# Four common steps of 208 columns in place of three of 256 between the forms of an attention and mixture-of-experts kernel

## The chip, the cores and the metric

The kernel runs on one core of a Trainium2 chip. The metric is device time in microseconds (us) of one execution, as the median of several runs. Engines are named as in the profile: PE is TensorE (PEld its weight loads), DVE is VectorE, ACT is ScalarE, POOL is GpSimd, SP is SyncE.

## What is computed

Attention of 4 x 8 heads over 768 positions with 64 numbers a head, with a window of 96 positions and 8 global ones, is followed by a top-1 routed mixture of 8 experts. All is float32. The second part matters here:

```
logits = x @ w_gate                      # x: 3072 tokens x 512
expert_idx = argmax(logits, axis=1)
for e in range(8):
    xe = x[expert_idx == e]
    h = maximum(xe @ w1[e], 0)           # w1[e]: 512 x 1024
    ye = h @ w2[e]                       # w2[e]: 1024 x 512
    out[expert_idx == e] = gate_w * ye
```

How many tokens an expert gets is known only when the kernel runs. With 3072 tokens it is 384 in the mean.

## The kernel before, in words

Every operation is first recorded in a list (`Flow.record`, L47), with what it reads and writes. `Flow.derive` finds from these which earlier operations each one must wait for, and `Flow.play` emits all of them in order, each on its engine's queue with its semaphore waits (`emit`, L239). The order within a queue is thus the order in which the Python code calls.

Attention runs over 24 blocks of 128 tokens and ends at about 205 us of the profile. Then come the experts, in the order 0, E, 1, 2, ..., 7. E is a late group of up to 128 tokens of expert 0, computed plainly (`plain`, L920).

**The two halves of an expert.** Up to 512 tokens of an expert are held as two halves of 256 columns each. Both matrix products are made as a 2 x 2 block product with seven block products in place of eight (`seven`, L836): `one`, `two`, `three`, `four`, `five`, `six`, `last`. Sums of weight blocks (`w_sums`, t1 to t4) and of token blocks (`x_sums`, `h_sums`) are made on DVE beforehand. `up` (L899) calls `seven` twice (j = 0 and 1, steps 0 to 6 and 7 to 13), `down` (L911) once (from step 14). A step writes one bank of PSUM: two column halves t times 2 (up) or 4 (down) blocks k, so 4 or 8 products, each 128 x 128 weights by up to 256 columns (`product`, L826).

After a step an engine takes the result out of PSUM: ACT copies `one` to p1 (L855); DVE adds p1 and `two` to u2 (L859); ACT activates `three` to block c11 (L864); DVE adds u2 and `four` to u3 (L870); DVE adds u3 and `five` to c22 (L874), u3 and `six` to c21 (L879), u2 and `last` to c12 (L884), and ACT activates these in place (L851). Banks come in two sets of three, X, Y and W, and consecutive calls of `seven` take turns: `one` and `three` write X, `two`, `four` and `six` write Y, `five` and `last` write W. So `four` waits until u2 has read Y, `six` until u3 has, and `last` until c22 has read W. Two more banks (`tbanks`) serve the transposes of `y_out`.

**Forms.** Columns past an expert's token count are wasted. So TensorE's instructions from a certain step on exist in 17 forms, for 128, 136, ..., 256 columns (`SIZES`, L636): `forms` opens such a section, and `emit_forms` (L269) writes it 17 times within a `Switch`, in which TensorE jumps to the form that fits. Only TensorE's instructions have forms; those of other engines are emitted once, for all 256 columns of each half. A form's products differ only in how many columns they take (`_dyn`, L257). A hint (`f.hint`) ahead of the section names the form that will be taken, and the branch itself is recorded at L275.

Between the end of one expert's form and the beginning of the next there is a **common part**, without forms and so with all 256 columns. In `group` (L1207), for each of the experts 1 to 7, it holds in this order: the hint; the loads of the next expert's rows (SP); `one`; two `y_out` of the expert before (4 transposes on TensorE each, then a scaling on ACT, then a send by POOL); `two`; two more `y_out`; `three`. Expert 1 has only one `y_out` there, since the late group precedes it. Then the form begins with `four`.

Other work is attached to steps with `at_(i, ...)` and is recorded after step i: weight sums on DVE after steps 0 and 1 (`own[3]`, `own[4]`, `own[5]`; L702, L699, L700), `pads` of the expert after the next after step 3 (four indirect DMAs on POOL, L744), the next weights' DMAs (SP) from step 14 on. Token sums of the next expert and its `marks` are recorded at the very end of an expert, so that on DVE they, and the two sums of step 0, stand ahead of u2.

Of the kernel before, what the change touches and what calls it, by code (L numbers as in the profile page):

```python
# [24 lines left out]
class Flow:  # L25
# [5 lines left out]

    RINGS = {"SP": 24, "POOL": 20, "ACT": 8}

    def __init__(self, tc):
# [9 lines left out]

    def record(self, engine, name, args, kw):  # L47
        reads, writes = list(kw.pop("_r", ())), list(kw.pop("_w", ()))
        dyn = kw.pop("_dyn", False)
        first = True  # L50
        for key, a in [(None, a) for a in args] + list(kw.items()):
            if not isinstance(a, bass.AP):
                first = first and key is not None
                continue
            if a.space == bass.MemoryType.DRAM:
                first = False
                continue
            (writes if key in ("out", "accum_out") or (key is None and first) else reads).append(a)
            first = False
        here = sys._getframe(2)  # L60
        self.ops.append(dict(e=engine, name=name, args=args, kw=kw, r=reads, w=writes, dyn=dyn,
                             form=self.form, dma="dma" in name,
                             at=(here.f_code.co_filename, here.f_lineno)))

# [171 lines left out]
        for j in op["need"]:  # L236
            self.engines[op["e"]].wait_ge(sems[self.ops[j]["proc"]], self.ops[j]["level"])

    def emit(self, op, sems, n):  # L239
        self.wait(op, sems)  # L240
        args, kw = op["args"], op["kw"]
        if op["name"] == "await":
            return
        if op["name"] == "number":
            ap, label = args
            self.loads[label] = self.nc.values_load(
                ap, min_val=0, max_val=1, skip_runtime_bounds_check_because="a comparison's result")
            return
        if op["name"] == "load":
            index, n, label = args  # L250
            self.loads[label] = self.nc.tensor.value_load(index, min_val=0, max_val=n - 1)
            return
        if op["name"] == "hint":
            index, n, label = args
            self.hints[label] = self.loads[label], self.nc.tensor.switch_hint(self.loads[label], n, label)
            return
        if n is not None and op["dyn"]:  # L257
            args = tuple(a[:, 0:n] for a in args[:1]) + tuple(args[1:])
            kw = dict(kw, rhs=kw["rhs"][:, 0:n])
        call = getattr(self.engines[op["e"]], op["name"])  # L260
        where = dict(call=call, args=args, kw=kw)

        exec(_code(*op["at"]), where)
        if op["dma"]:
            where["inst"].then_inc(sems[op["proc"]], 16)
        elif op.get("told"):
            where["inst"].then_inc(sems[op["proc"]], 1)

    def emit_forms(self, form, body, sems):  # L269
        index, sizes, label = form  # L270
        pe = self.nc.tensor
        choose, rest = body[0], body[1:]
        self.wait(choose, sems)
        r, label = self.hints[label]
        for f in pe.Switch(r, len(sizes), hint=label):  # L275
            for op in rest:
                self.emit(op, sems, sizes[f])


class _Recorder:  # L280
# [344 lines left out]
class Experts:  # L625
# [6 lines left out]

    P, E, CAP, LATE = 128, 8, 512, 128
    SIZES = list(range(128, 257, 8))  # L636

    def __init__(self, f, dims, psum, keep, wsets, work, zeros, ylast):
# [149 lines left out]
    def bank(self):  # L788
        self.tp ^= 1
        return self.psum[:, self.tbanks[self.tp], :].rearrange("p (c t) -> p c t", c=4)  # L790
# [32 lines left out]
            in_=self.y[j], in_offset=None, bounds_check=self.out.shape[0] - 1, oob_is_err=False, **kw)  # L823


    def product(self, bank, w, x, fresh, half=None):  # L826

        f, n = self.f, len(w)
        for t in range(2):
            for k in range(n):  # L830
                f.pe.matmul(self.psum[:, bank, 256 * t:256 * t + 256], lhsT=w[k][:, ts(t, 128)], rhs=x[k],  # L831
                            start=(fresh and t == 0 and k == 0), stop=True, skip_group_check=True, _dyn=True)
            if half and t == 0:
                half()

    def seven(self, c, a, s, cols, order, dst, act, half=None):  # L836

        f, V = self.f, self.f.dve
        X, Y, W = self.sets[self.turn]
        p1, u2, u3 = self.p1[self.turn], self.u2[self.turn], self.u3[self.turn]  # L840
        self.turn ^= 1

        def bank(b):
            return self.psum[:, b, :].rearrange("p (t c) -> p t c", t=2)

        def mm(b, wq, xq, fresh, half=None):
            self.product(b, [c[wq][:, k, cols] for k in order], [xq[:, k, :] for k in order], fresh, half)

        def relu(d):
            if act:  # L850
                f.act.activation(d, d, act)  # L851

        def one():
            mm(X, "b11", a["a11"], True)
            f.act.copy(p1, bank(X))  # L855

        def two():
            mm(Y, "t2", s[1], True)
            V.tensor_tensor(u2, p1, bank(Y), ALU.add)  # L859

        def three():
            mm(X, "b21", a["a12"], False, half)
            if act:
                f.act.activation(dst["c11"], bank(X), act)  # L864
            else:
                f.act.copy(dst["c11"], bank(X))

        def four():
            mm(Y, "t3", s[2], True)
            V.tensor_tensor(u3, u2, bank(Y), ALU.add)  # L870

        def five():
            mm(W, "t1", s[0], True)
            V.tensor_tensor(dst["c22"], u3, bank(W), ALU.add)  # L874
            relu(dst["c22"])

        def six():
            mm(Y, "t4", a["a22"], True)
            V.tensor_tensor(dst["c21"], u3, bank(Y), ALU.add)  # L879
            relu(dst["c21"])  # L880

        def last():
            mm(W, "b22", s[3], False)
            V.tensor_tensor(dst["c12"], u2, bank(W), ALU.add)  # L884
            relu(dst["c12"])

        return [one, two, four, five, six, three, last] if half else [one, two, three, four, five, six, last]

    def h_sums(self, j):
        V, sh = self.f.dve, self.sh  # L890
# [8 lines left out]
    def up(self, e):  # L899

        c, xt, h = self.quarters(e, True), self.xt, self.h
        a = dict(a11=xt[:, 0:2, 0], a12=xt[:, 2:4, 0], a21=xt[:, 0:2, 1], a22=xt[:, 2:4, 1])
        s = [self.sx[:, j] for j in range(4)]
        steps = []
        for j in range(2):
            k, k2 = slice(2 * j, 2 * j + 2), slice(4 + 2 * j, 6 + 2 * j)
            dst = dict(c11=h[:, k, 0], c12=h[:, k2, 0], c21=h[:, k, 1], c22=h[:, k2, 1])
            steps += self.seven(c, a, s, slice(256 * j, 256 * j + 256), (0, 1), dst, AF.Relu)
        return steps

    def down(self, e, half=None):  # L911
# [32 lines left out]
def kernel(  # L944
# [60 lines left out]
    with ExitStack() as stack:  # L1005
# [201 lines left out]
        def group(p):  # L1207
# [6 lines left out]
            def at_(i, *fns):  # L1214
                todo.setdefault(i, []).extend(fns)

            def run(steps, first):
                for i, fn in enumerate(steps, first):
                    fn()
                    for fn in todo.pop(i, ()):  # L1220
                        fn()

            ups = ex.up(g) if g != E else None
            if p:

                prev = order[p - 1]
                if E not in (g, prev):
                    f.hint(*forms[g])
                if nxt is not None and g != E:
                    ex.load_x(nxt, [f"pad{nxt}.{j}" for j in range(4)])  # L1230
                if nxt is None:
                    f.number(keep["flag"][0:1, 0:1], "redo")
                outs = [0] if prev == E else [1, 3, 0, 2]
                own = ex.w_sums(g, True) + ex.w_sums(g, False) if ups else None
                if ups:
                    at_(0, own[3], own[4])
                    at_(1, own[5])
                    run(ups[:1], 0)
                for j in outs[:2]:
                    ex.y_out(prev, j)  # L1240
                if ups:
                    run(ups[1:2], 1)
                for j in outs[2:]:
                    ex.y_out(prev, j)
                if ups:
                    run(ups[2:3], 2)
            D = 14
            if g != E:

# [39 lines left out]
            else:  # L1289
# [7 lines left out]
                    at_(D + 6, xs[2], xs[3], lambda: ex.marks(nxt))  # L1297
                if after is not None:
                    pieces = ex.w_pieces(after)
                    at_(3, lambda: ex.pads(after))  # L1300
                    at_(D, *pieces[:4])
                    at_(D + 6, *pieces[4:])

# [1 line left out]
                ex.plain(0, lambda i: [fn() for fn in todo.pop(i, ())])  # L1305
                return
            with f.forms(*forms[g]):
                run(ups[3:] if p else ups[2:], 3 if p else 2)
                early = ((1, "act"), (3, "dve")) if nxt is None else ()
                run(ex.down(g, (lambda: [ex.y_out(g, j, on) for j, on in early]) if early else None), D)  # L1310
            assert not todo, todo
# [432 lines left out]
```

## Time and profile before

| | |
|---|---|
| median of 14 runs | 513.77 us (512.78 to 514.45) |
| the profiled execution | 514.43 us, its span 512.6 us |
| TensorE's mean granted clock | 0.985 |
| busy: POOL | 164.8 us (32%) |

By stages, from the view of busy times in windows, in us:

| stage (us) | length | PE | DVE | ACT | POOL | DMA share |
|---|---|---|---|---|---|---|
| 223.5 to 264.4, expert 1 | 40.90 | 40.90 | 25.75 | 8.29 | 5.54 | 0.75 |
| 264.4 to 302.5, expert 2 | 38.10 | 38.10 | 29.32 | 9.65 | 8.77 | 0.67 |
| 302.5 to 343.3, expert 3 | 40.80 | 40.80 | 29.33 | 9.76 | 9.17 | 0.61 |
| 343.3 to 381.4, expert 4 | 38.10 | 38.10 | 29.39 | 9.65 | 9.41 | 0.66 |
| 381.4 to 423.5, expert 5 | 42.10 | 42.10 | 29.32 | 9.76 | 9.38 | 0.60 |
| 423.5 to 464.25, expert 6 | 40.75 | 40.75 | 29.33 | 9.76 | 5.07 | 0.29 |
| 464.25 to 499.4, expert 7 | 35.15 | 33.55 | 23.71 | 10.80 | 6.32 | 0.09 |
| 499.4 to 512.6, the end | 13.20 | 0.00 | 0.74 | 0.22 | 1.94 | 0.08 |

How to read the lines that follow: a group names the line, the engine, the operation, what it writes and reads, the shape and the count; then busy time and the mean of one in ns; then the idle time ahead of it and what ended most of that. One product in float32 leaves two matmul records. A matmul's length is modelled and overlaps the next, so the pace is read from starts.

### The profile page before, as it was taken

Reading aid. Unit: us, or ns where it says so; the run is one execution under the profiler, and the core shown is the slowest. Engines: PE = TensorE matmul, PEld = TensorE weight load, DVE = VectorE, ACT = ScalarE, POOL = GpSimd, SP = SyncE. Lnnn points to the kernel's source line nnn. Section 1 sums busy time; section 2 is a strip of 40 time slices with the busy share of each in tenths; the row PEclk is TensorE's granted clock in tenths of the full one; section 3 lists DMA queues with packets and bytes.
Section 4 is the critical chain, followed back from the end, with each engine's and each line's share of the span. In section 5 each row is a group of like instructions: output and inputs, shape, how many; then the busy total and the mean of one; then the engine's idle time right before and its main releaser. Section 6 shows DMA issues by size and latency. Waiting matters only on the chain. (4 is left out here: it accounts for less than half of the span.)

```text
span 512.6 us, 10727 instructions
## 1 busy us (share of the span) xinstructions
PE 481.2 (94%) x4397; PEld 452.6 (88%) x4397; DVE 350.7 (68%) x612; ACT 171.8 (34%) x292; POOL 164.8 (32%) x192
## 2 busy tenths in 40 slices
PE   3999999999986999999999999999999999999990
PEld 3888888888875899899999999999999999999880
DVE  4655675897885785566777886777876776777840
ACT  3766655555552130312113213204213203302410
POOL 1544456667765053322006006007007003003011
PEclk9999999999999799999999999999999999999996
DMA  9999999998425347998756665657567469001000
GB/s 151 206 241 253 195 201 239 262 223 185 104 103 126 131 158 149 203 241 206 164 187 155 142 211 137 130 170 178 134 195 183 108 161 231 2 2 59 9 24 29
DMA packets 120344, 79.24 MB, mean 155 GB/s; under 512 B 86422, under 2 KB 103318, under 8 KB 120272
## 3 DMA queue, kind: packets, MB, share of 16 engines
q1 hardware_dynamic: 112960, 63.77, 56.6%
q0 software_dynamic: 6480, 14.45, 7.9%
q8 instruction: 51, 0.84, 0.7%
q14 instruction: 21, 0.17, 0.1%
q10 hardware_dynamic: 832, 0.02, 0.1%
HBM read 61.39 MB, written 23.71 MB: 166 GB/s over the span
## 5 line engine op out<-in xcount | busy, mean ns | idle before, releaser
L831 PE MATMUL psum<-arena 128*128 128x208 f32 (+5 forms) x1776 | 298.3, 329 | 5.0 <-DVE arena L795 4.1
L831 PEld LDWEIGHTS psum<-arena 128*128 128x128 f32 x1776 | 287.6, 191 | 10.5 <-DVE arena L795 4.2
L821 POOL DMA_INDIRECT out_dram<-arena,to x16 | 20.8, 1297 | 214.9 <-ACT arena L813 189.9
L491 DVE TENSOR_TENSOR arena<-psum,arena 128x1024 f32<-128x1024 f32 x40 | 48.8, 1219 | 30.9 <-PE psum L481 30.9
L499 ACT ACTIVATE arena<-arena 128x1024 f32<-128x1024 f32 (+1 forms) x48 | 47.4, 987 | 46.6 <-DVE arena L491 42.0
L505 POOL TENSOR_TENSOR arena<-arena 128x512 f32<-128x512 f32 x40 | 53.2, 1332 | 29.7 <-ACT arena L499 29.7
L851 ACT ACTIVATE arena<-arena 128x512 f32<-128x512 f32 x48 | 30.2, 630 | 63.5 <-DVE arena L874 43.2
L481 PE MATMUL psum<-arena 64*128 64x128 f32 x704 | 48.5, 284 | 1.2 <-ACT arena L467 0.7
L481 PEld LDWEIGHTS psum<-arena 64*128 64x128 f32 x704 | 43.4, 191 | 5.8 <-issue 3.2
L855 ACT COPY arena<-psum 128x512 f32<-128x512 f32 x24 | 14.0, 584 | 90.1 <-PE psum L831 90.0
L518 PE MATMUL psum<-arena 128*64 128x128 f32 x704 | 43.7, 276 | 0.3 <-issue 0.3
L518 PEld LDWEIGHTS psum<-arena 128*64 128x64 f32 x704 | 37.9, 137 | 3.2 <-issue 0.4
L870 DVE TENSOR_TENSOR arena<-arena,psum 128x512 f32<-128x512 f32 x24 | 16.5, 688 | 27.0 <-PE psum L831 26.9
L617 POOL DMA_INDIRECT xg_dram<-arena,slot_i x24 | 24.6, 1027 | 29.4 <-DVE arena L884 21.8
L744 POOL DMA_INDIRECT xg_dram<-small,pad x24 | 25.5, 1061 | 12.5 <-issue 7.0
L884 DVE TENSOR_TENSOR arena<-arena,psum 128x512 f32<-128x512 f32 x24 | 16.5, 688 | 17.6 <-PE psum L831 17.6
L874 DVE TENSOR_TENSOR arena<-arena,psum 128x512 f32<-128x512 f32 x24 | 16.5, 688 | 16.7 <-PE psum L831 16.7
L879 DVE TENSOR_TENSOR arena<-arena,psum 128x512 f32<-128x512 f32 x24 | 16.5, 688 | 15.2 <-PE psum L831 15.2
L821 POOL DMA_INDIRECT out_dram<-ylast,to x17 | 17.3, 1015 | 22.7 <-ACT ylast L813 14.6
L457 PE MATMUL psum<-ident,arena 128*128 128x128 f32 x96 | 16.1, 294 | 8.7 <-DMA arena<-in_k_dram 7.2
L859 DVE TENSOR_TENSOR arena<-arena,psum 128x512 f32<-128x512 f32 x24 | 16.4, 685 | 11.1 <-PE psum L831 10.7
L699 DVE TENSOR_TENSOR arena<-arena 128x1024 f32<-128x1024 f32 x16 | 19.6, 1227 | 2.8 <-DMA arena<-in_moe_w_dram 2.8
(148 smaller groups left out, 529.1 us busy)
## 6 DMA issues: line engine op xcount, KB each, us to landing
arena<-in_moe_w_dram SPq DMA_DIRECT2D x64, 512.0 KB, 5.6
arena<-xg_dram SPq DMA_DIRECT2D x64, 128.0 KB, 6.1
arena<-in_q_dram SPq DMA_DIRECT2D x24, 256.0 KB, 5.7
arena<-in_k_dram SPq DMA_DIRECT2D x24, 256.0 KB, 5.7
arena<-in_v_dram SPq DMA_DIRECT2D x24, 256.0 KB, 5.8
xg_dram<-arena SPq DMA_DIRECT2D x2, 1032.0 KB, 5.7
xg_dram<-arena,slot_i POOLq DMA_INDIRECT x24, 4.2
xg_dram<-small,pad POOLq DMA_INDIRECT x24, 3.2
```

Of the source, the lines that this page charges most:

```text
L481: f.pe.matmul(self.psum[:, 2 * g + a, c:c + P], lhsT=kt[r, m, :], rhs=qt[r, m, :], start=True, stop=True, skip_group_check=True)
L491: f.dve.tensor_tensor(e, s, self.bias[:, g, :, 1:3, :].rearrange("p h k c -> p h (k c)"), ALU.add)
L499: f.act.activation(e, e, AF.Exp)
L505: f.pool.tensor_tensor(self.es[n % 3][:, g], e[:, :, 0:P], e[:, :, P:2 * P], ALU.add)
L518: f.pe.matmul(po[r, m, :], lhsT=self.v[(n - ab) % 6][:, 2 * m + a, :], rhs=self.e[n % 2][:, m // 2, 2 * a + m % 2, P * ab:P * ab + P], sta ...
L617: self.f.pool.indirect_dma_start(out=self.xs[:], out_offset=bass.IndirectOffsetOnAxis(ap=k["slot_i"][:, b % 2, u:u + 1], axis=0), in_=self ...
L699: return [lambda: V.tensor_tensor(c["t3"], c["b22"], c["b12"], ALU.subtract), lambda: V.tensor_tensor(c["t1"], c["b12"], c["b11"], ALU.sub ...
L744: self.f.pool.indirect_dma_start(out=self.xs[:], out_offset=bass.IndirectOffsetOnAxis(ap=self.keep["pad"][:, g, j:j + 1], axis=0), in_=sel ...
L821: return pool.indirect_dma_start(out=self.out[:], out_offset=bass.IndirectOffsetOnAxis(ap=self.keep["to"][:, g, j:j + 1], axis=0), in_=sel ...
L831: f.pe.matmul(self.psum[:, bank, 256 * t:256 * t + 256], lhsT=w[k][:, ts(t, 128)], rhs=x[k], start=(fresh and t == 0 and k == 0), stop=Tru ...
L851: f.act.activation(d, d, act)
L870: V.tensor_tensor(u3, u2, bank(Y), ALU.add)
```

## The change

The common part gets `four` as its fourth step, and its four steps take the first 208 columns (`COMMON`) of each half. A form with more columns than 208 begins with `rest`: the products of `one`, `two`, `three` and `four` for the columns past 208, into banks of the other set and one of the transposes' banks. In a form of up to 208 these products are left out (`_past`); what they would have told other engines is told by the next product that is emitted (`more`). The other engines have no forms: for the columns 208 to 255 ACT makes one more copy and one more activation, and DVE two more additions, in every expert from 1 on, and they are recorded ahead of `five`. Expert 0, the second call of `seven` in `up` and the call in `down` stay as they were. `pads` are attached to step 4 in place of step 3.

```diff
@@ record
-        dyn = kw.pop("_dyn", False)
+        dyn, past = kw.pop("_dyn", False), kw.pop("_past", 0)
@@ emit(self, op, sems, n, more=0)
         if n is not None and op["dyn"]:
+            n -= op["past"]
             args = tuple(a[:, 0:n] for a in args[:1]) + tuple(args[1:])
             kw = dict(kw, rhs=kw["rhs"][:, 0:n])
...
-        elif op.get("told"):
-            where["inst"].then_inc(sems[op["proc"]], 1)
+        elif op.get("told") or more:
+            where["inst"].then_inc(sems[op["proc"]], int(bool(op.get("told"))) + more)
@@ emit_forms
         for f in pe.Switch(r, len(sizes), hint=label):
+            more = 0
             for op in rest:
-                self.emit(op, sems, sizes[f])
+                if op["past"] and sizes[f] <= op["past"]:
+                    self.wait(op, sems)
+                    more += bool(op.get("told"))
+                    continue
+                self.emit(op, sems, sizes[f], more)
+                more = 0
@@ Experts
-    P, E, CAP, LATE = 128, 8, 512, 128
+    P, E, CAP, LATE, COMMON = 128, 8, 512, 128, 208
@@ product(self, bank, w, x, fresh, half=None, cut=slice(0, 256))
-                f.pe.matmul(self.psum[:, bank, 256 * t:256 * t + 256], lhsT=w[k][:, ts(t, 128)], rhs=x[k],
-                            start=(fresh and t == 0 and k == 0), stop=True, skip_group_check=True, _dyn=True)
+                f.pe.matmul(self.psum[:, bank, 256 * t + cut.start:256 * t + cut.stop], lhsT=w[k][:, ts(t, 128)],
+                            rhs=x[k][:, cut], start=(fresh and t == 0 and k == 0), stop=True,
+                            skip_group_check=True, _dyn=True, _past=cut.start)
@@ seven(..., half=None, common=False)
+        X2, Y2, W2 = self.sets[self.turn ^ 1]
+        some, past = slice(0, self.COMMON if common else 256), slice(self.COMMON, 256)
...
         def one():
-            mm(X, "b11", a["a11"], True)
-            f.act.copy(p1, bank(X))
+            mm(X, "b11", a["a11"], True, cut=some)
+            f.act.copy(p1[:, :, some], bank(X)[:, :, some])
...
         def four():
-            mm(Y, "t3", s[2], True)
-            V.tensor_tensor(u3, u2, bank(Y), ALU.add)
+            mm(Y, "t3", s[2], True, cut=some)
+            V.tensor_tensor(u3[:, :, some], u2[:, :, some], bank(Y)[:, :, some], ALU.add)
+
+        def rest():
+            T = self.tbanks[self.tp ^ 1]
+            mm(X2, "b11", a["a11"], True, cut=past)
+            f.act.copy(p1[:, :, past], bank(X2)[:, :, past])
+            mm(Y2, "t2", s[1], True, cut=past)
+            V.tensor_tensor(u2[:, :, past], p1[:, :, past], bank(Y2)[:, :, past], ALU.add)
+            mm(W2, "b11", a["a11"], True, cut=past)
+            mm(W2, "b21", a["a12"], False, cut=past)
+            f.act.activation(dst["c11"][:, :, past], bank(W2)[:, :, past], act)
+            mm(T, "t3", s[2], True, cut=past)
+            V.tensor_tensor(u3[:, :, past], u2[:, :, past], bank(T)[:, :, past], ALU.add)
...
-        return [one, two, four, five, six, three, last] if half else [one, two, three, four, five, six, last]
+        if half:
+            return [one, two, four, five, six, three, last]
+        if common:
+            return [one, two, three, four, lambda: [rest(), five()], six, last]
+        return [one, two, three, four, five, six, last]
@@ up
-            steps += self.seven(c, a, s, slice(256 * j, 256 * j + 256), (0, 1), dst, AF.Relu)
+            steps += self.seven(c, a, s, slice(256 * j, 256 * j + 256), (0, 1), dst, AF.Relu,
+                                common=(e > 0 and j == 0))
@@ group
                 if ups:
-                    run(ups[2:3], 2)
+                    run(ups[2:4], 2)
...
-                    at_(3, lambda: ex.pads(after))
+                    at_(4, lambda: ex.pads(after))
...
-                run(ups[3:] if p else ups[2:], 3 if p else 2)
+                run(ups[4:] if p else ups[2:], 4 if p else 2)
```

`two` and `three` change as `one` does.

## The prediction

> **What bounds the kernel now.** I read the page's part 1 and part 2 first, then the matmul group of its part 5, to see which engine the time belongs to.
>
> ```profile
> PE 481.2 (94%) x4397; PEld 452.6 (88%) x4397; DVE 350.7 (68%) x612; ACT 171.8 (34%) x292; POOL 164.8 (32%) x192
> ...
> PE   3999999999986999999999999999999999999990
> ...
> L831 PE MATMUL psum<-arena 128*128 128x208 f32 (+5 forms) x1776 | 298.3, 329 | 5.0 <-DVE arena L795 4.1
> ```
>
> TensorE is busy in every slice, and the expert products of L831 are most of it. They waited 5.0 us in all, 4.1 of it in the first expert, which the change doesn't touch. So time here is TensorE's pace times its columns. TensorE's granted clock is 1.00 in each of these stretches. The pace comes from starts in the timeline of TensorE from 225 us on (start, length, what, records; a merged line bears the shape of its first record). One product is two records, so a step of 4 products in the up half is 8 records.
>
> ```profile
> 267.00 1.89 PE L831 MATMUL psum<-arena 128*128 128x256 f32 x8
> 268.73 1.04 PE L810 MATMUL psum<-ident,arena 128*128 128x128 f32 x8
> 269.60 34.82 PE L831 MATMUL psum<-arena 128*128 128x256 f32 x216
> 304.25 1.04 PE L810 MATMUL psum<-ident,arena 128*128 128x128 f32 x8
> ...
> 386.59 38.78 PE L831 MATMUL psum<-arena 128*128 128x256 f32 x216
> 425.21 1.04 PE L810 MATMUL psum<-ident,arena 128*128 128x128 f32 x8
> ```
>
> A step of 256 columns takes 268.73 - 267.00 = **1.73 us** (216 ns a record). The stretch 269.60 to 304.25 is `three`, 200 records in the form and the next expert's `one`: (34.65 - 2 x 1.73) / 200 = 156 ns. In the same way 386.59 to 425.21 gives 176 ns, and the stretch between these, 307.73 to 345.02, 169 ns. Which width each form has is in the groups with shapes kept apart; over experts 1 to 7 these are
>
> ```profile
> L831 PE MATMUL psum<-arena 128*128 128x208 f32 x400 | 70.7, 339 | 0.0
> L831 PE MATMUL psum<-arena 128*128 128x200 f32 x400 | 68.0, 332 | 0.0
> L831 PE MATMUL psum<-arena 128*128 128x184 f32 x400 | 62.7, 319 | 0.0
> L831 PE MATMUL psum<-arena 128*128 128x136 f32 x200 | 24.7, 283 | 0.9 <-DVE arena L859 0.8
> ```
>
> Each expert has 200 records in its form, so two experts run at 208 columns, two at 200, two at 184, one at 136 (116 ns a record: 24 records from 494.68 to 497.46). In order they are 208, 184, 200, 184, 208, 200, 136. **No form is over 208**: on this data TensorE never runs the new part for the columns past 208. Only what goes with it on ACT and DVE runs.
>
> **The change, part by part.**
>
> TensorE. Each of experts 1 to 7 has three common steps of 256 and `four` in its form; afterwards it has four common steps of 208. A step of 208 costs 8 x 176 ns = 1.41 us. Saved per expert: 3 x 1.73 + 8 x (pace of its form) - 4 x 1.41. At 208 that is 5.19 + 1.41 - 5.62 = 0.97; at 200, 0.92; at 184, 0.81; at 136, 0.49. The sum is 2 x 0.97 + 2 x 0.92 + 2 x 0.81 + 0.49 = **5.9 us**, all of it on the path, since TensorE has no idle time in these stretches to give it back to.
>
> `four` in the common part. It writes the bank that `u2` (L859) reads, and now comes sooner after it. These are DVE's lines ahead of the third expert's switch (start, length, what):
>
> ```profile
> 304.93 1.22 DVE L702 TENSOR_TENSOR arena<-arena 128x1024 f32<-128x1024 f32 x1
> 306.07 1.22 DVE L699 TENSOR_TENSOR arena<-arena 128x1024 f32<-128x1024 f32 x1
> 307.21 0.68 DVE L859 TENSOR_TENSOR arena<-arena,psum 128x512 f32<-128x512 f32 x1
> ```
>
> `u2` starts behind two weight sums, not behind TensorE, so it doesn't move with TensorE. It gets 0.1 us shorter (416 elements in place of 512; 1024 take 1.22 and 512 take 0.69, so 1.04 ns each over 0.16 fixed) and ends at 307.80. `one` began at 302.52 (304.25 - 1.73), so `four` will be due at 302.52 + 3 x 1.41 + 2 x 0.87 (transposes, 269.60 - 268.73) = 308.48: 0.7 us of slack. In the second expert `u2` starts at 269.79 and ends at 270.38, where `four` is due at 264.39 + 5.96 = 270.35: a wait of about **0.1 us** with the hand-over. In the seventh (469.51) the two meet within 0.1 us. Behind a waiting `four` TensorE has the switch and all of the form.
>
> Pieces of 48 columns. One copy and one activation on ACT, two additions on DVE per expert, and they run whatever the form is. By the slope above a piece of 96 elements costs DVE 0.26; ACT has 0.37 for 256 elements (L939) and 0.58 for 512 (L855), so 0.24 for 96. For forms up to 208 they wait for the first product of `five`, and `c22` (L874) waits behind them on DVE. From the start of `five`: 2 records, 0.20 hand-over (ACT's L864 starts at 309.66, TensorE's next step at 309.46), 0.24, 0.26, 0.26 and three hand-overs of 0.03. That is 1.3 us at 136 columns and up to 1.4 at 208. `c22` must anyway wait for all of `five`, 8 records and 0.20: 1.13 at 136, 1.45 at 184, 1.61 at 208. So the chain is hidden, except in the seventh expert: **0.15 us**. There the next but one step (`last`) waits for `c22`, so I charge it. If the pieces cost twice as much, the experts of 184 lose up to 0.3 each on `c22`, but `last` has more than that in hand.
>
> `pads` go from behind step 3 to behind step 4. Between these points POOL has nothing else queued and SP nothing either, so neither order changes: nothing. Cover if wrong: the padded rows are first read by loads that the next expert issues. Weights and rows are loaded as before, one expert about 0.9 us sooner; DMA is 9% to 75% busy by stage, and no wait of L831 from the second expert on is for a DMA.
>
> The switch. This is the cost I can't read off directly. The rows of L275 (min/median/max in ns) are
>
> ```profile
> L275 PEldq COMPARE_BRANCH  x16: 292/303/2462, 172.9 to 495.4; - x16
> ...
> L275 PEldq BRANCH_PREFETCH_HINT  x8: 40/45/45, 173.3 to 468.8; - x8
> ```
>
> The branch into the form is reached some 18 records ahead of TensorE. It takes 0.3 us where the code is there, but 1.53 to 2.46 us in experts 2 to 6: in the third from 306.71 to 309.17, with `four` at 309.46. An instruction transfer begins before each of these (306.48 in the third, 426.65 against a branch at 427.67 in the sixth), 5.0 to 5.6 us behind the transfer before it, and the branch ends 2.6 to 2.9 us after the transfer's start. So the code's arrival hangs on the exit from the last form, not on the branch. After the change it is needed at 302.52 + 7.36 = 309.88, later by 0.4 us than now: covered. What is uncertain is whether TensorE's sequencer can pass the weight load of `four` while that waits for `u2`. If it can, the cost is 0. If it can't, it must issue 32 instructions, the table look-up (0.27) and the branch (0.30, and 0.20 to the first weight load) after `u2`. At most 25 ns an instruction (L518: 32 loads and 32 matmuls in 1.6 us), with 0.06 for the hand-over, that is 1.63 us: 307.80 + 1.63 = 309.43, still in time in the third, some 0.25 late in the second and the seventh. Bounds 0 to 0.5 us; I take 0, since the sequencer's lead of 18 records is the same at all entries and exits, whatever waits were in it.
>
> The Trainium skill speaks on both sides here. "Runtime: NRT & Kernel Launch", Instruction fetch mechanics, says that a taken branch whose target isn't in the present window stops for a fetch; the branches of 2.4 us agree, and by it alone each of five experts would be open to 2.2 us more. "Perfetto Trace Analysis", on TensorE instructions, says that a waiting instruction sits in a queue and the sequencer goes on; by that the hold costs nothing. No row of this trace shows a branch behind a waiting load, so it doesn't decide.
>
> **Sum.** -5.9 + 0.1 + 0.15 = -5.6 us. The profiled execution has 514.43 with a span of 512.6; it becomes 508.8. The median shown is 513.77, 0.66 below that execution, so I predict **508.2**.
>
> **The rivals.**
>
> *The sequencer is held (part of the gain is lost).* As above, but with slower issue. The mean over the common part is 80 instructions between 301.24 and 306.44, 65 ns, though there it ran against a full queue. At 45 ns the 32 instructions take 1.44 in place of 0.8 us: about 0.3 us late in experts 1 and 3 to 6, 0.9 in 2 and 7, so 3.3 lost, 511.3. For it: `u2` ends only 0.7 us ahead of `four`. Against it: 25 ns from L518. Its range is 509.5 to 512.5.
>
> *The code comes late (slower).* If the transfer of the form's code starts only when the branch is reached, and that is held behind `u2`, experts 2 to 6 pay 2.15 us more (2.45 - 0.30): in the third 309.43 + 2.15 = 311.58, where it is needed at 309.78, so 1.8 late; four of these, 2.4 in the second and 0.2 in the seventh are 9.8, against 5.6: 4.2 us slower, 518. It decides against the change from about 1.2 us of lateness per expert. Against it: the transfers that start before the branch.
>
> *It saves less because `c22` and `last` lag.* If ACT and DVE pieces take twice my figures, the seventh expert loses all of its 0.49 and the 184s some tenths: 509.
>
> *It doesn't do what it says.* If a form over 208 were taken, 20 more products would run; the groups show none.
>
> **How the numbers follow.** Forecast, with the third rival in it: 68%, own range 507.6 to 509.5. Sequencer held: 20%. Change below 0.2%, where delays eat almost all: 5%. Code late: 7%. The range 507.6 to 512.0 leaves out some 15%. A measurement here tells about 0.2% (1.0 us) from no change: faster 0.88, same 0.05, slower 0.07.
>
> **What would show it.** Right: groups of 8 records at 208 columns, 1.41 us apart, 32 per expert, and none narrower than 128; idle time of L831 under 1 us more than now; branches of L275 still ending before the form's first product. Wrong: TensorE idle ahead of `five` in each expert, with "issue" as its end (sequencer or code), or L859 as the cause of idle time in more than two experts.

## The result and the profile after

| | before | after |
|---|---|---|
| median | 513.57 us (28 runs, 512.30 to 514.88) | 507.39 us (6 runs, 506.87 to 508.66) |
| ratio of the medians | | 0.9884, 95% interval 0.9873 to 0.9896 |
| profiled execution, its span | 514.43, 512.6 | 508.07, 506.2 |

The changed kernel is faster by 6.2 us. The page of its profile, parts 1, 2 and 5, in the same order as before:

```profile
PE 474.8 (94%) x4397; PEld 450.5 (89%) x4397; DVE 352.2 (70%) x626; ACT 173.9 (34%) x306; POOL 165.9 (33%) x192
...
PE   3999999999987899999999999999999999999990
...
L842 PE MATMUL psum<-arena 128*128 128x208 f32 (+5 forms) x1776 | 293.1, 326 | 4.9 <-DVE arena L806 4.0
```

TensorE lost 6.4 us of busy time with the same number of matmuls, and the products (now L842) wait as little as before. DVE and ACT have 14 instructions more each, the pieces of 48 columns. The timeline of TensorE gives the new pace (start, length, what, records):

```profile
266.02 1.04 PE L821 MATMUL psum<-ident,arena 128*128 128x128 f32 x8
266.90 34.31 PE L842 MATMUL psum<-arena 128*128 128x208 f32 x216
301.04 1.04 PE L821 MATMUL psum<-ident,arena 128*128 128x128 f32 x8
301.91 1.57 PE L842 MATMUL psum<-arena 128*128 128x208 f32 x8
303.32 1.04 PE L821 MATMUL psum<-ident,arena 128*128 128x128 f32 x8
```

A step of 208 columns takes 303.32 - 301.91 = 1.41 us, where one of 256 took 1.73. The groups with shapes kept apart, over experts 1 to 7, show which widths ran:

```profile
L842 PE MATMUL psum<-arena 128*128 128x208 f32 x604 | 109.7, 339 | 0.0
L842 PE MATMUL psum<-arena 128*128 128x200 f32 x384 | 65.3, 332 | 0.0
L842 PE MATMUL psum<-arena 128*128 128x184 f32 x384 | 60.2, 319 | 0.0
...
L842 PE MATMUL psum<-arena 128*128 128x136 f32 x192 | 23.9, 283 | 0.9 <-DVE arena L874 0.8
```

A form now has 192 records, since `four` left it, and the 208 columns have 7 x 32 records of the common parts beside 2 x 192 of forms (four less in this view, whose window begins at 223.5 us, within expert 1's `one`). No group is narrower than 128: `rest` never ran.

**Where the time went.** I call **head** the time from the first record of `one` to the first record of `six`. It holds everything that the change touches on TensorE. By expert, in us:

| | 1 | 2 | 3 | 4 | 5 | 6 | 7 | sum |
|---|---|---|---|---|---|---|---|---|
| before | 8.44 | 9.45 | 9.64 | 9.42 | 9.75 | 9.64 | 8.80 | 65.14 |
| after | 7.47 | 8.62 | 8.73 | 8.91 | 8.78 | 9.02 | 8.33 | 59.87 |
| after less before | -0.97 | -0.83 | -0.91 | -0.51 | -0.97 | -0.62 | -0.47 | -5.27 |

From the start of expert 1 to the last product the two executions differ by -5.17 us: the heads, less 0.1 us that expert 7 loses after `six`. The rest of the 6.2 us lies ahead of expert 1, which begins at 223.61 before and at 222.50 after. The change doesn't touch that part. In other profiles of the two kernels it begins between 223.0 and 225.8, so I take that 1.1 us for chance; no run shows what set it.

Experts 4 and 6 got 0.3 us less than their widths promise. The waits of TensorE's weight loads name who they waited for (total, times, longest):

```profile
PEld psum L842 <- DVE arena L874: 1.9, 4, 1.1
```

L874 is `u2`. The same row of the kernel before, where `u2` is L859, is

```profile
PEld psum L831 <- DVE arena L859: 1.3, 2, 1.1
```

Two waits, 0.6 us, are new. To see why, DVE's timeline in expert 4, whose `one` starts at 339.49:

```profile
341.69 0.16 DVE L796 TENSOR_TENSOR to<-to,inv_i 128x4 int32<-128x4 int32 x1
342.73 1.22 DVE L713 TENSOR_TENSOR arena<-arena 128x1024 f32<-128x1024 f32 x1 [0.88 <-issue]
343.87 1.22 DVE L710 TENSOR_TENSOR arena<-arena 128x1024 f32<-128x1024 f32 x1
345.01 0.58 DVE L874 TENSOR_TENSOR arena<-arena,psum 128x416 f32<-128x416 f32 x1
```

and the weight loads of TensorE there:

```profile
345.64 2.02 PEld L842 LDWEIGHTS psum<-arena 128*128 128x128 f32 x12 [0.34 <-DVE arena L874]
```

DVE begins the first of the two weight sums (L713) 0.88 us late, with nothing in the profile to wait for ("issue"). `u2` therefore ends at 345.59, 6.10 us after `one`, where it ends at 5.26 in experts 3 and 5. `four` is due at 5.96, so it starts late. Before the change such a gap stood in experts 2 (0.76) and 7 (0.62); after it, in 2 (0.55), 4 and 6 (0.88 each) and 7 (0.62).

### The profile page after: what moved, and what is told of

Read it like the earlier page. It is cut to its first block, busy times and chain, and to the rows that moved or that the text cites. A ratio compares the mean times of both kernels' runs of the same rounds, so it can differ in the third digit from the quotient of the medians.

```text
span 506.2 us, 10775 instructions
## 1 busy us (share of the span) xinstructions
PE 474.8 (94%) x4397; PEld 450.5 (89%) x4397; DVE 352.2 (70%) x626; ACT 173.9 (34%) x306; POOL 165.9 (33%) x192
## 5 line engine op out<-in xcount | busy, mean ns | idle before, releaser
L842 PE MATMUL psum<-arena 128*128 128x208 f32 (+5 forms) x1776 | 293.1, 326 | 4.9 <-DVE arena L806 4.0
L842 PEld LDWEIGHTS psum<-arena 128*128 128x128 f32 x1776 | 286.5, 191 | 7.5 <-DVE arena L806 4.2
L870 ACT COPY arena<-psum 128x512 f32<-128x512 f32 (+1 forms) x24 | 13.4, 559 | 87.8 <-PE psum L842 87.7
L885 DVE TENSOR_TENSOR arena<-arena,psum 128x512 f32<-128x512 f32 (+1 forms) x24 | 15.8, 659 | 21.6 <-PE psum L842 21.5
L911 DVE TENSOR_TENSOR arena<-arena,psum 128x512 f32<-128x512 f32 x24 | 16.5, 688 | 17.8 <-PE psum L842 17.8
L906 DVE TENSOR_TENSOR arena<-arena,psum 128x512 f32<-128x512 f32 x24 | 16.5, 689 | 15.1 <-PE psum L842 14.9
L901 DVE TENSOR_TENSOR arena<-arena,psum 128x512 f32<-128x512 f32 x24 | 16.5, 688 | 13.7 <-PE psum L842 13.6
L874 DVE TENSOR_TENSOR arena<-arena,psum 128x512 f32<-128x512 f32 (+1 forms) x24 | 15.8, 656 | 10.0 <-PE psum L842 9.6
L713 DVE TENSOR_TENSOR arena<-arena 128x1024 f32<-128x1024 f32 x16 | 19.9, 1243 | 3.0 <-issue 2.9
```

What stands on the lines that cost most here:

```text
L713: lambda: V.tensor_tensor(c["t4"], c["b21"], c["t2"], ALU.subtract)]
L842: f.pe.matmul(self.psum[:, bank, 256 * t + cut.start:256 * t + cut.stop], lhsT=w[k][:, ts(t, 128)], rhs=x[k][:, cut], start=(fresh and t = ...
```

## The experiments

The kernels ran on three other chips than the first comparison, e1 to e4 on one, e5 to e8 on the next, e9 and e10 on the third. There the kernel before has medians of 519.51 (516.56 to 524.77, 23 runs), 519.74 (517.42 to 522.30, 25) and 516.97 (515.53 to 519.43, 12), more widely spread than on the first chip. Part of the spread lies in the forms, as e6 shows. So the theories are judged by heads, and medians stand beside them.

| kernel | sum of heads | median (range) | ratio to before, interval |
|---|---|---|---|
| e5, e9: the changed kernel | 59.87, 59.88 | 517.74 (514.38 to 522.19), 513.22 (510.93 to 516.88) | 0.9950 (0.9929 to 0.9970), 0.9914 (0.9880 to 0.9948) |
| e6: the kernel before | 65.39 | 518.98 (516.23 to 525.57) | 0.9983 (0.9960 to 1.0006) |
| e1: `four` moved, 256 wide | 68.25 | 522.11 (520.83 to 523.65) | 1.0061 (1.0038 to 1.0084) |
| e2: three steps of 208 | 63.44 | 519.10 (516.60 to 522.54) | 1.0001 (0.9971 to 1.0031) |
| e3, e7, e10: one sum later | 59.28 each | 516.30, 516.25, 512.45 | 0.9935 (0.9907 to 0.9963), 0.9906 (0.9872 to 0.9940), 0.9914 (0.9882 to 0.9945) |
| e4: no pieces | 59.82 | 513.97 (513.84 to 514.36) | 0.9906 (0.9882 to 0.9931) |
| e8: 192 columns | 83.73 | 544.15 (543.23 to 553.04) | 1.0473 (1.0443 to 1.0504) |

**e1, one half of the change alone: `four` in the common part, at 256 columns.**

```diff
-    P, E, CAP, LATE, COMMON = 128, 8, 512, 128, 208
+    P, E, CAP, LATE, COMMON = 128, 8, 512, 128, 256
-            return [one, two, three, four, lambda: [rest(), five()], six, last]
+            return [one, two, three, four, five, six, last]
```

> Four common steps, but of 256 columns, so that `four` is moved into the common part and nothing is narrowed; no work for columns past the common width is left. Theory (TensorE's columns times its pace, nothing else): `four` costs 1.73 us in place of 8 records at the form's pace, that is 0.32 us more in each of two experts of 208, 0.38 in two of 200, 0.48 in two of 184 and 0.80 in the one of 136, 3.2 in all over the kernel before: 516.7 us against 513.6. Rival (the move itself brings part of the gain, since the form's code has longer to arrive): at or below 513.6.

The heads sum to 68.25, 3.11 more than before, where 3.2 was expected; the rival, a gain from the move itself, is refuted. The group of the common steps carries it:

```profile
L842 PE MATMUL psum<-arena 128*128 128x256 f32 x224 | 51.6, 379 | 0.0
```

224 records are 7 x 32, at 216 ns each, without idle time. So moving `four` alone makes the kernel slower by the columns that a form would have left out, and the whole gain is the narrower width.

**e2, the other half alone: three common steps of 208, `four` in the form.**

```diff
-            return [one, two, three, four, lambda: [rest(), five()], six, last]
+            return [one, two, three, lambda: [rest(), four()], five, six, last]
-                    run(ups[2:4], 2)
+                    run(ups[2:3], 2)
-                    at_(4, lambda: ex.pads(after))
+                    at_(3, lambda: ex.pads(after))
```

(`rest` loses its fourth product, `four` takes all columns of its form again, and the form begins at step 3.)

> Three common steps of 208 columns, `four` back in the form; only the narrowing is made. By columns alone each of seven experts saves 3 x 0.32 = 0.97 us: 6.8 in all, 506.8 us. Theory with a limit by the form's code: in the changed kernel the branch into the form could end 6.1 to 6.65 us after the start of `one` in experts 2 to 6; here the form is due 5.87 us after it, so TensorE stands still 0.2 to 0.8 us in each of these, 2.4 in all: 509.2 us, with idle time ahead of `four` ended by issue. Rival (the code comes sooner when it is asked for sooner, no limit): 506.8 us and no such idle time.

By columns the heads should sum to 58.4; they sum to 63.44, so 5.0 us are lost. The view of waits of the weight loads, the switch's rows, and TensorE's timeline in the third expert say how:

```profile
PEld psum L842 <- issue: 5.2, 5, 1.2
```

```profile
L277 PEldq COMPARE_BRANCH  x16: 292/306/2954, 173.8 to 499.2; - x16
```

```profile
307.58 1.57 PE L842 MATMUL psum<-arena 128*128 128x208 f32 x8
310.05 1.25 PE L842 MATMUL psum<-arena 128*128 128x200 f32 x6 [0.90 <-issue]
```

Five times, in experts 2 to 6, TensorE runs dry at the end of the common part, and each time the branch takes 2.57 to 2.95 us. The branches end 6.37 to 6.71 us after the start of `one`, as in the kernel before (5.72 to 6.65) and in those two experts of the changed one, 3 and 5, in which the branch waits for the code (6.65 and 6.56), although the form is now due at 5.9. The transfers of instructions in the traces say the same: the one ahead of the form begins 3.7 to 4.0 us after `one` here, 3.2 to 4.1 before and 3.5 to 4.0 in the changed kernel, while the branch begins at 3.7 to 3.8, 4.2 and 5.6 to 6.4. So in these three kernels the code's arrival doesn't move with the branch. That it hangs on the exit from the last form fits this, but no run moves that exit alone. The mechanism is as expected, and its price about twice as high (5.0 for 2.4), since the arrivals lie at the late end and TensorE's first product comes another 0.26 to 0.32 us after the branch. **`four` in the common part is what covers the code.** The change needs both halves: one alone costs 3.1 us, the other one gives back 5.0 of its 6.7.

**e3, the cause of the new wait: one weight sum less ahead of `u2`.**

```diff
-                    at_(0, own[3], own[4])
-                    at_(1, own[5])
+                    at_(0, own[3])
+                    at_(1, own[4], own[5])
```

> The changed kernel with one weight sum of 1.22 us (the first of the down part) recorded on DVE behind u2 in place of ahead of it. Theory (the 0.3 us that experts 4 and 6 lose ahead of `four`, and what little 7 loses, is the wait for u2, late behind DVE's two sums): u2 ends about 1.1 us sooner, `four` waits in no expert, 0.6 us less than the changed kernel: 506.8 against 507.4 us, and the branch into the form is reached sooner after the start of `one`. Rival (the 0.3 us are the switch's own, the code or the branch): experts 4 and 6 as before, 507.4 us.

The heads sum to 59.28, 0.59 below the changed kernel: 8.62 and 8.73 in experts 4 and 6. DVE in the fourth expert:

```profile
348.11 1.23 DVE L713 TENSOR_TENSOR arena<-arena 128x1024 f32<-128x1024 f32 x1 [0.87 <-issue]
349.25 0.58 DVE L874 TENSOR_TENSOR arena<-arena,psum 128x416 f32<-128x416 f32 x1
349.75 1.22 DVE L710 TENSOR_TENSOR arena<-arena 128x1024 f32<-128x1024 f32 x1
```

The gap of 0.87 us is still there, but `u2` now follows one sum, and `four` doesn't wait for it. So `four` waited because of what DVE had queued ahead of `u2`, and the 0.59 is what that cost. Why DVE begins late remains open.

**e4, the pieces: `rest` is left out.** The columns 208 to 255 of the first four products are then never computed, so this kernel leaves that part out.

```diff
-            return [one, two, three, four, lambda: [rest(), five()], six, last]
+            return [one, two, three, four, five, six, last]
```

> The changed kernel without any work for columns 208 to 255 in the first four products: neither the products in forms over 208 nor the four small instructions on ACT and DVE; these columns are left out of the computation. Theory (the pieces are hidden in all experts but the seventh, where c22 waits for them): 0.1 to 0.15 us less, 507.3 us, with c22 in the seventh expert starting 1.13 us after the start of `five` in place of 1.28. Rival (the pieces hold up TensorE in more experts, through c22 and the accumulation behind it): 0.3 us an expert, 505.5 us.

This one is only partly clean. In expert 7 the part from the start of `six` to the last product is 0.08 us shorter than after. The heads sum to 59.82, about the same as after, but by other parts: DVE's gap is gone from experts 4 and 6 and has grown from 0.55 to 0.76 in expert 2, which costs 0.17, and in expert 5 the branch ended 7.42 us after `one`, which costs 0.36. Where neither happens (1, 3) the heads are 7.47 and 8.73 with and without the pieces. What the pieces could delay is `c22`, behind the head; from the start of `five` it starts at the same time with and without them in experts 1, 2, 3, 4 and 6 (1.68, 1.52, 1.62, 1.52, 1.62 us). So they are hidden there; expert 5, where the code came late, doesn't tell.

**e5 and e6, the two kernels again on the second chip.** No edit.

> The changed kernel again, beside the others of this set on one chip. In the first set, on another chip than the changed kernel's own, TensorE stood still for up to 3 us in the forms of experts 2 to 4, at ACT's first copy of the second half of `up`, in all four kernels; that has to be kept apart from what the change does. Theory: with those stalls taken out, experts 1 to 7 are 5.2 us shorter than before, and the ratio to before is again 0.987 to 0.990. Rival (those stalls come of the changed kernels' own order): they are absent in the kernel before on this chip, and the ratio is above 0.993.

> The kernel before again, with its profile on the same chip as the others of this set. Theory: a ratio of 1; if the chip has the stalls at ACT's copy in experts 2 to 4, this kernel has them too. Rival: it has none while the others have.

The heads of the changed kernel repeat to 0.01 us in every expert, so the losses in experts 4 and 6 are no accident of one execution. The kernel before has 65.39: 0.27 more in expert 5, where the branch ended late. The medians are less apart than on the first chip: e5 is 2.0 us below the kernel before, and its ratio of 0.9950 misses the expected 0.987 to 0.990, though by heads it is 5.5 us below e6. The view of waits of TensorE in e6 shows one reason (total, times, longest):

```profile
PE psum L831 <- ACT arena L855: 3.8, 2, 1.9
```

and the timeline of one of these places, in the kernel before:

```profile
278.73 0.69 DVE L884 TENSOR_TENSOR arena<-arena,psum 128x512 f32<-128x512 f32 x1 [2.21 <-PE psum L831]
...
280.82 2.45 PE L831 MATMUL psum<-arena 128*128 128x184 f32 x14 [1.89 <-ACT arena L855]
```

DVE takes out `last` 2.2 us later than TensorE's records would let it, and ACT's copy (L855) and TensorE come late behind it. Such stalls occur in forms of both kernels on these chips, and not in the first two profiles, so they don't come of the change alone. But they aren't alike: experts 1 to 7 are 4.7 us longer in e6 than in the first profile of the kernel before, and 8.0 and 8.6 us longer in e5 and e9 than in the first profile of the changed kernel. With one such profile of the kernel before, it isn't shown whether the change makes them longer. What delays the hand-over from TensorE is not settled.

**e7, e9 and e10: one sum later beside the changed kernel, twice.** No new edit.

> The first weight sum of the down part behind u2, measured beside the changed kernel on the same chip. In the first set `four` waited in none of its experts. Theory: 0.6 us less than the changed kernel where DVE is late in two experts, 0.1 to 0.3% at most, which the medians may not tell; in the profile u2 ends 0.7 to 1.2 us sooner after the start of `one`. Rival (the wait only moves to u3 and `six`): no gain, with TensorE idle ahead of `six`.

> The changed kernel once more, for the median and the profile. The stretch from the start of `one` to the start of `six`, summed over experts 1 to 7, was 65.14 and 65.39 us in two profiles of the kernel before and 59.87 in two of the changed kernel. Theory: 59.87 again, with experts 4 and 6 at 8.91 and 9.02; where the forms of experts 2 to 5 are undisturbed, as they were in the changed kernel's first profile, the median is 0.987 to 0.990 of before. Rival (the ratio of 0.995 in the second set is the change's true size): 0.993 or more even in undisturbed forms.

> The changed kernel with the first weight sum of the down part behind u2, once more. Theory: the same stretch sums to 59.28 us as in its two earlier profiles, and the median is 0.1 to 0.3% below the changed kernel's. Rival (what is saved ahead of `four` is given back later in the expert): the same stretch is 59.28, but the lengths of the experts are those of the changed kernel.

The heads are 59.28 in both runs against 59.87 and 59.88, so the 0.59 us is shown. It isn't given back later: of the two experts that had the wait, expert 6 has an undisturbed form in all three runs with the later sum, and as a whole it takes 39.85 or 39.86 us there, 40.14 in the first profile of the changed kernel. The medians are 1.5 us (e7 under e5) and 0.8 us (e10 under e9) lower, but the intervals overlap, and so medians don't tell the two apart. By its heads this is the best version tried: 59.28 in each of three profiles, on three chips. On the chip of e3 the changed kernel was not run beside it. The ratio of e9, 0.9914, lies between its theory and its rival, but its forms were disturbed, so the theory's condition wasn't met.

**e8, the part that this data never runs: `COMMON` of 192, so that forms of 200 and 208 run `rest`.**

```diff
-    P, E, CAP, LATE, COMMON = 128, 8, 512, 128, 208
+    P, E, CAP, LATE, COMMON = 128, 8, 512, 128, 192
```

> The changed kernel with a common width of 192 columns in place of 208, so that the four experts of 200 and 208 run the part for the columns past it: 20 products, 40 records, of 8 or 16 columns. The four common steps get 4 x 8 x 13.4 ns = 0.43 us shorter in each of seven experts, 3.0 in all. Theory (a narrow product costs its weight load, not its columns; nearest rows: 18 ns a record with 32 weight columns, 51 ns with 64, 109 ns for a transpose with 128): 50 to 110 ns a record, 2.0 to 4.4 us an expert, 8 to 17.6 in all, so 5 to 14.6 us slower than the changed kernel. Rival (cost by columns alone, 7 to 13 ns a record): 1.6 us in all, 1.4 us faster than the changed kernel.

4.7% slower than before, and 26.4 us slower than the changed kernel on this chip (e5), where 5 to 14.6 was expected; 23.9 of it lies in the heads. The new groups, over experts 1 to 7:

```profile
L842 PE MATMUL psum<-arena 128*128 128x8 f32 x80 | 10.7, 275 | 0.0
L842 PE MATMUL psum<-arena 128*128 128x16 f32 x80 | 9.1, 261 | 0.0
```

By starts, a record takes 111 ns at 8 columns as at 16, so the 40 records of `rest` cost 4.4 us per expert, however few columns they hold. That is 17.6 us for four experts, the upper end of what was expected. What the expectation lacked is lost to the form's code, late in experts 2 and 7 (TensorE dry for 1.5 and 3.1 us; the branches end 8.3 and 10.0 us after `one`), and to a lower clock. This is the view of windows about the third expert (window, length, busy time of PE, PEld, DVE, ACT and POOL, granted clock, DMA share, GB/s):

```profile
314.00:316.70 2.70, 2.70 (x26) 2.70 (x24) 0.56 (x1) 0.00 (x0) 2.09 (x3) 1.00 1.17 308
316.70:323.60 6.90, 6.90 (x29) 6.90 (x29) 0.80 (x3) 0.54 (x2) 3.29 (x4) 0.51 0.31 87
```

At a clock of 0.51 half as many records pass, and `rest` takes 6.0 us there in place of 4.4. From these numbers I estimate that in the changed kernel an expert with a form of 216 would lose about 3.4 us against the kernel before: `rest` costs 4.4 and the four steps of 208 cost 5.6, where, in the kernel before, the three of 256 cost 5.2 and `four` at 216 would cost 1.45 (8 records of 181 ns, between 176 and 216). No run here has such data.

## Why the prediction held, point by point

- **Pace.** Right. Forecast were 5.9 us without waits; where the new wait is gone (e3, e7 and e10, 59.28) the heads are 5.86 shorter than before. Experts 1, 3 and 5 gained 0.97, 0.91 and 0.97.
- **`four` behind `u2`.** Right in kind, wrong in place and size: 0.1 was charged in expert 2; measured are 0 there, 0.29 each in experts 4 and 6 and 0.02 in 7. The step took `u2` from where DVE had it before. But DVE's late start, which stood in experts 2 and 7, is in 2, 4, 6 and 7 after (0.55 to 0.88 us), and `four` has no slack for the 0.88 in 4 and 6. The forecast had named more than two experts as the sign of an error; `four` waits in two.
- **Pieces and `c22`.** Right. A piece took DVE 0.254 us and ACT 0.238 and 0.257 (forecast 0.26 and 0.24). In expert 7 `c22` starts 1.28 us after `five`, 1.20 without the pieces; the cost is 0.08, where 0.15 was charged.
- **The switch.** The price of 0 was right, the reason for it wrong. The prediction held that the sequencer keeps its lead of 18 records, whatever waits ahead. It does not: the first rival's mechanism is real. In experts 1 to 7 of the changed kernel the first instruction of the switch starts 0.072 us after the end of `u2` each time:

| expert | `u2` ends | switch starts | branch ends | `four` was due, the form is due |
|---|---|---|---|---|
| 3 | 304.89 | 304.97 | 306.28 | 305.59, 307.0 |
| 4 | 345.59 | 345.66 | 346.32 | 345.45, 347.1 |
| 7 | 464.19 | 464.27 | 464.83 | 464.32, 465.7 |

In e3, where `u2` ends before `four` is due, it is the same 0.072 (349.833 and 349.905). In the kernel before, the switch started 0.8 us *before* `u2` began in experts 3 and 4 (306.44 against 307.21 in 3) and 1.3 us before it in 7. What was wrong in the rival is the price: it had 32 instructions to issue after `u2`, and the trace shows only the table look-up and the branch between, 0.64 us in all where the code is there (expert 7). `four` itself then runs for 1.41 us, which covers that. The switch's rows say the same from the other side; the longest branch is now 1.04 us, where it was 2.46:

```profile
L277 PEldq COMPARE_BRANCH  x16: 296/302/1042, 172.6 to 489.1; - x16
```

- **The code.** Right, with little to spare: the form is due 7.4 us after `one`. In experts 3 and 5, where the branch waits for the code, it ends at 6.65 and 6.56; in 2, 4, 6 and 7 it takes 0.30 to 0.39 us, so the code is there already. In other runs with this common part it ended as late as 7.04 (e9) and 7.42 (e4, where it cost 0.36), both in expert 5. e2 shows the price where there is no cover. The rival in which the transfer waits for the branch is refuted by the changed kernel: the transfers begin 1.6 to 2.9 us ahead of the branches of experts 2 to 6, and the longest branch is 1.04 us. (That rival's sum takes 309.78 for the time of need in the third expert, where the prediction worked out 309.88; its lateness there is 1.7 us, not 1.8.)
- **`pads`, DMAs, queues.** Nothing to see, as forecast: no new wait names them.
- **The sum.** Forecast -5.6, measured -5.2 in the experts; in the profiled executions the rest lies in unaltered work ahead of expert 1, for which the forecast had no term. So a part of how close 508.2 came to 507.39 is luck. The chip of the first comparison was luck as well: on two others the medians of the changed kernel are only 2.0 and 3.8 us below the kernel before, with the stalls of unsettled cause in the forms. What repeats is the gain in the heads: 59.87 or 59.88 in all three profiles of the changed kernel, against 65.14 and 65.39 in the two of the kernel before.

## What to carry to other kernels

Price a change of columns by the pace between starts in a stretch without idle time: it came out to 0.01 us. Before work is moved between a common part and a section whose code must be fetched, ask for how long the common part must last to cover the code; here the width gave the gain, and the moved step paid for the cover. And look at what the queue of the releasing engine holds ahead of the release: one sum of 1.2 us in the wrong place there decided over 0.3 us in each of two experts.

## What the runs showed of the hardware

- TensorE's sequencer did not pass a weight load that waits for a semaphore: the first instruction of the switch behind it began 0.071 to 0.074 us after the end of `u2`, in every expert from 1 on in all nine profiles with `four` in the common part.
- A float32 product with 8 or 16 columns took nearly as long (111 ns a record, e8) as one with 136 (116 ns).
- After some stalls the granted clock fell to half for about 3.4 us: in e5 after 2.35 us without a product (from 362.2 to 365.6: 306 ns a record where 156 is usual) and in e9 after 2.77. In e3 a longer stall, 2.85 us, left it at 1.00, so the length alone does not decide. e8 has stretches of half clock of 3.4 to 6.9 us.
- DVE started 0.55 to 0.97 us late after a branch of its own in some experts. Which ones depends on the kernel: 2 and 7 before, in e1 and in e4; 2, 4, 6 and 7 after, in e2 and in e3. That its code came late there is a guess; no run tested it.
